# First attention chunk of a block loaded six units ahead, chunks cut at block ends, outputs held in a free buffer

## The chip, the cores and the metric

The kernel runs on one core of one Trainium2 chip. The time is the device time of one execution, in microseconds (us). Five engines work side by side, each with its own queue that it takes in order: PE (TensorE, matmuls; PEld is its weight load), DVE (VectorE), ACT (ScalarE), POOL (GpSimd) and SP (SyncE, which here only starts DMAs).

## The reference

Attention on 4 batches x 8 heads x 576 positions x 64 in two parts that are added: a dense attention on means of four positions (144 x 144), and a local one in which each position sees the 7 positions around it. The result, 2304 tokens x 512, goes through two feed-forward nets:

```python
out_d = sm_attn(q_d, k_d, v_d)             # means of 4 positions
mask = np.abs(pos[:, None] - pos[None, :]) < 4
x = np.repeat(out_d, 4, axis=2) + sm_attn_masked(q, k, v, mask)
g = x @ w_gate; x = (g * sigmoid(g) * (x @ w_val)) @ w_out      # d_ff 1536
h = x @ w_in;   x = (h * clip(h + 3, 0, 6) / 6) @ w_out2         # d_ff 2048
```

## The kernel before

**Blocks and units.** The 2304 tokens are 36 groups of 64, nine to a batch, and `BLOCKS = [8, 6, 8, 8, 6]` cuts them into five blocks, B0 to B4 below. Each block goes through the same 68 units (`NU`), one per 128 columns of a weight matrix: 36 of the first net (G, V, and O which sums into x2), then 32 of the second (H, and P which sums into the output). `run_unit` (L873) issues a unit's matmuls: each weight and each activation is split into a high and a low part, so a unit has 12 matmuls (9 for a P unit of a 6-group block). The first 36 units are called the first half of the block, the other 32 the second half.

**Weights.** `prefetch(i)` (L215) keeps them coming: a load 8 units ahead in B0 (from the 8-byte inputs, turned to f32 by `decode_a` on ACT and `decode_b` on DVE, and written back to DRAM as `kept`), 6 units ahead in later blocks (from `kept`), and two units ahead `split_unit` (L206): ACT writes the high part `wr`, then DVE the low part (in B1 every fourth one is POOL's). The loads sit in SP's queue.

**Attention of the next block beside the nets of this one.** Batch 0 is done before everything else by `first_batch`. The rest of the local attention is done in chunks of 3 groups (`CT = 12` positions of each of 16 x 8 segments), nine of them, on DVE: `chunk_scores` (L726) has two large instructions per group (the product `pr` L731, the sum L734) and a few small ones per chunk; then one Exp on ACT; then `unit_values` (L752) per group: the product `pv` L766 and three sums L770 to L772, with four small instructions ahead of a chunk's first group. `step_x` (L777) turns a group's result on PE and DVE adds the dense part to it (`xf` L796). `CHUNKS = [2, 3, 2, 2, 0]` says how many chunks a block begins: 6, 9, 6, 6 and 0 groups. A block's values must reach to the end of the next block (`limit`), that is 5, 8, 8 and 6 groups; values left over are done first in the next block. Scores are spread over a block's first half, values over the second (`sizes`, L1000). The means for the dense part of the next batch are summed on POOL in the first half (`down_sums` L262, two buffers), its matmuls are in the second half.

**Order.** The program is written unit by unit, but the framework's planner orders each engine's queue from its own estimate of the durations, so work on DVE can come well before its place in the program. DMAs issued through `late` keep their order on SP. A chunk's q, k and v are loaded by `load_chunk` (L690), the first at unit 0 of its block and the second at unit 4 (`CLOAD`), later ones after the scores of the chunk two before. k has 2 buffers, v 3.

**Outputs.** The last P unit ends four sums (three in a 6-group block); `put_out` (L945) copies each from PSUM to one of two buffers `os`, ACT and DVE in turn, and SP writes it out. The third copy waits until the first output has landed.

**Constants.** Two small masks, `ones_last`, are made on POOL and DVE right after `first_batch` (L667 to L685), in a pool that takes over the memory of `first_batch`.

Of the kernel before, what the change touches and what calls it, by code (L numbers as in the profile page):

```python
# [10 lines left out]
F32 = mybir.dt.float32  # L11
# [29 lines left out]
def tile_kernel(  # L41
# [25 lines left out]
    UT = 4 * NSEG  # L67
    CT = 12
    SUB = 4
    NCH = SL // CT  # L70
    UPC = CT // 4
    BS = H * S * D
# [24 lines left out]
    half1 = cp.tile([P, 1], F32, name="half1")  # L97
    nc.gpsimd.memset(half1, 0.5)

    def flat(ap, off, dims):  # L100
# [565 lines left out]
    ap = ctx.enter_context(tc.tile_pool(name="ap", bufs=2))  # L666
    ones_last = []  # L667
    for side in range(2):
        ih = ap.tile([P, H], F32, tag=f"ih{side}", name=f"ih{side}", bufs=1)
        nc.gpsimd.memset(ih, 0.0)  # L670
        nc.gpsimd.affine_select(
            out=ih, in_=ih, compare_op=ALU.not_equal, fill=NEG,
            base=-(NSEG - 1) * side, pattern=[[-NSEG, H]], channel_multiplier=1,
        )
        ind = ap.tile([P, 1], F32, tag=f"ind{side}", name=f"ind{side}", bufs=1)
        nc.vector.tensor_reduce(ind, ih, axis=AX.X, op=ALU.add)
        on = ap.tile([P, 4, W], F32, tag=f"on{side}", name=f"on{side}", bufs=1)
        nc.gpsimd.memset(on, 0.0)
        sgn = 1 if side == 0 else -1
        nc.gpsimd.affine_select(  # L680
            out=on, in_=on, compare_op=ALU.is_ge, fill=1.0,
            base=-3 if side == 0 else 6, pattern=[[sgn, 4], [sgn, W]], channel_multiplier=0,
        )
        nc.vector.tensor_scalar(on, on, ind[:, 0:1], None, op0=ALU.mult)
        ones_last.append(on)  # L685

    odT = {}
    kvq = {}

    def load_chunk(b, c):  # L690
        t0 = c * CT
        qt = ap.tile([P, CT, D], F32, tag="qt", name=f"q{b}_{c}")
        late(nc.sync, qt, flat(q, b * BS + t0 * D, [[PS, P], [1, CT * D]]).rearrange("p (t d) -> p t d", d=D))
        res = [qt]
        NT = CT + 6
        for nm, src in (("k", k), ("v", v)):
            kt = ap.tile([P, NT, D], F32, tag=nm + "t", name=f"{nm}{b}_{c}", bufs=2 if nm == "k" else 3)
            base = b * BS + (t0 - 3) * D

            def ld(p0, p1, r0, r1, shift=0):  # L700
                late(
                    nc.sync, kt[p0:p1, r0:r1, :],
                    flat(src, base + p0 * PS + r0 * D + shift, [[PS, p1 - p0], [1, (r1 - r0) * D]]).rearrange(
                        "p (t d) -> p t d", d=D
                    ),
                )

            if b == B - 1 and c == NCH - 1:
# [16 lines left out]

    def chunk_scores(b, c):  # L726
        qt, kt, vt = kvq.pop((b, c))
        sc = ap.tile([P, CT, W], F32, tag="sc", name=f"sc{b}_{c}", bufs=3)
        for a in range(0, CT, SUB):
# [8 lines left out]
        if c == NCH - 1:  # L738
            nc.vector.tensor_tensor(sc[:, CT - 4:CT], sc[:, CT - 4:CT], ones_last[1], op=ALU.add)
        mx = ap.tile([P, CT], F32, tag="mx", name=f"mx{b}_{c}")  # L740
        nc.vector.tensor_reduce(mx, sc, axis=AX.X, op=ALU.max)
        nc.vector.tensor_tensor(sc, sc, mx[:, :, None].to_broadcast([P, CT, W]), op=ALU.subtract)
        pes[b, c] = sc, vt

    def chunk_exp(b, c):
        sc, _ = pes[b, c]
        nc.scalar.activation(sc, sc, AF.Exp, scale=0.125)
# [4 lines left out]
    def unit_values():  # L752

        b, c, i = vq.popleft()
        pe, vt = pes[b, c]
        if i == 0:
            sm = ap.tile([P, CT], F32, tag="sm", name=f"sm{b}_{c}")
# [3 lines left out]
            nc.vector.tensor_tensor(pe, pe, sm[:, :, None].to_broadcast([P, CT, W]), op=ALU.mult)  # L761
            os_[b, c] = ap.tile([P, CT, D], F32, tag="o", name=f"o{b}_{c}", bufs=3)
# [9 lines left out]
        nc.vector.tensor_tensor(o[:, a:a + SUB], pr[:, :, 0], pr[:, :, 1], op=ALU.add)  # L772
        xq.append((b, c, i, o))
        if i == UPC - 1:
            del pes[b, c], os_[b, c]

    def step_x(limit):  # L777

        if not xq or xq[0][0] not in down_done or xq[0][0] * NG + xq[0][1] * UPC + xq[0][2] >= limit:
            return  # L780
        b, c, i, o = xq.popleft()
        u = c * UPC + i
        gu = b * NG + u
# [177 lines left out]

    chunks = [(b, c) for b in range(1, B) for c in range(NCH)]
    assert sum(CHUNKS) == len(chunks)
    at = 0
# [8 lines left out]
    for bi in range(NB):  # L973
        mine = chunks[at:at + CHUNKS[bi]]
        at += len(mine)
# [13 lines left out]
        def second_half():  # L989
            for ch in mine:  # L990
                chunk_exp(*ch)
                vq.extend((*ch, i) for i in range(UPC))
# [6 lines left out]
        done = (at - len(mine)) * UPC  # L999
        sizes = [len(vq) + len(mine) * UPC, max(min(limit - NG, at * UPC) - done, 0)]  # L1000
        main = iter(())
# [5 lines left out]
        for i in range(bi * NU, (bi + 1) * NU):  # L1007
# [60 lines left out]
```

## Time and profile before

| | |
|---|---|
| median of 3 runs | 1026.6 us (1026.35 to 1028.46) |
| the profiled execution: its time, its span | 1027.78 us, 1025.7 us |
| mean granted TensorE clock | 0.982 of full speed |
| busy share of the span: PE, PEld, DVE, ACT, POOL | 95%, 78%, 77%, 52%, 14% |
| instructions on PE, DVE, ACT, POOL | 4798, 1251, 1070, 130 |
| moved by DMA | 159.92 MB, mean 156 GB/s |

Busy shares are means over the whole span. The five blocks have different limits: the first unit of B1 starts at 283.88 us, of B2 at 464.08, of B3 at 680.80 and of B4 at 874.59, and the second half of B1 at about 380, of B2 at about 578, of B3 at 784. In a row, "idle before <-X" in square brackets is how long the engine stood still before the instruction and whose end released it.

### The profile page before, as it was taken

To read this page: it belongs to the slowest core of one execution; us is meant where nothing else is said; L and a number is where in the kernel's file an instruction comes from. 1 tells how busy PE (TensorE), PEld (TensorE's weight loads), DVE (VectorE), ACT (ScalarE), POOL (GpSimd) and SP (SyncE) were. 2 spreads that over 40 slices of the span, in tenths; PEclk is the share of its full clock that TensorE was granted. 3 is DMA by queue.
4 is the path that set the end of the run, shared out by engine and by line. 5 is a ranking of instruction groups with operands and counts; after the bars stand their busy time and mean duration, and the time that the engine had idled before them with its cause. 6 is when DMAs were issued, how large, how long until landed. Compare 5 with 4: busy or idle time off the path is not lost.

```text
span 1025.7 us, 13478 instructions
## 1 busy us (share of the span) xinstructions
PE 969.7 (95%) x4798; PEld 800.8 (78%) x4800; DVE 789.5 (77%) x1251; ACT 530.9 (52%) x1070; POOL 139.1 (14%) x130
## 2 busy tenths in 40 slices
PE   7868999999997899998999999999999999999996
PEld 4556888777886897886767777777888888999995
DVE  6596999998789999996999765549995655545653
ACT  4684576776544456553344555444435444444553
POOL 5273000000057411211640000000000000000000
PEclk9789999999999899999999999999999999999999
DMA  8668988678486642236833322254223222533331
GB/s 163 175 206 299 332 294 274 210 253 264 143 274 166 181 127 100 102 104 167 234 117 103 103 69 75 82 177 172 91 94 103 82 103 86 161 123 124 126 126 46
DMA packets 82790, 159.92 MB, mean 156 GB/s; under 512 B 19364, under 2 KB 51620, under 8 KB 82724
## 3 DMA queue, kind: packets, MB, share of 16 engines
q1 hardware_dynamic: 77828, 141.25, 44.3%
q10 hardware_dynamic: 4896, 17.83, 4.7%
q8 instruction: 38, 0.62, 0.2%
q14 instruction: 28, 0.23, 0.1%
HBM read 136.51 MB, written 22.54 MB: 155 GB/s over the span
## 4 chain that ended last, share of the span: by engine, by line
PE 68%; DVE 17%; DMA 6%; issue 4%; POOL 2%; ACT 2%; SPq 0%; DVEq 0%; ACTq 0%; POOLq 0%
PE pH L887 19%; PE aP L929 17%; PE aO L929 11%; PE pG L887 9%; PE pV L887 9%; DVE wr L212 4%; DVE sc L734 2%; DVE pr L731 2%; DMA k<-in_k_dram 1%; PE pS L816 1%; DMA out_dram<-os 1%; DVE gV L905 1%; DMA nv<-in_v_dram 1%; DVE sl L899 1%; DVE xf L796 1%
## 5 line engine op out<-in xcount | busy, mean ns | idle before, releaser
L212 DVE TENSOR_TENSOR wr<-w,wr 128x512 fp32r<-128x512 f32 x323 | 234.4, 729 | 85.9 <-ACT wr L209 83.7
L209 ACT ACTIVATE wr<-w 128x512 fp32r<-128x512 f32 x340 | 211.5, 626 | 154.1 <-PE aP L929 68.3
L887 PE MATMUL pH<-x,wr 128*128 128x512 f32 (+1 forms) x960 | 216.1, 376 | 0.4 <-ACT x L942 0.3
L929 PE MATMUL aP<-wr,gH 128*128 128x512 f32 x864 | 213.5, 398 | 0.0
L887 PEld LDWEIGHTS pH<-x,wr 128*128 128x128 f32 x960 | 173.0, 188 | 29.5 <-issue 4.5
L929 PEld LDWEIGHTS aP<-wr,gH 128*128 128x128 f32 x864 | 159.5, 188 | 36.5 <-issue 1.9
L887 PE MATMUL pG<-xr,wr 128*128 128x512 f32 (+3 forms) x732 | 164.3, 378 | 19.5 <-DVE sl L899 14.2
L887 PEld LDWEIGHTS pG<-xr,wr 128*128 128x128 f32 x732 | 134.7, 192 | 43.2 <-issue 12.6
L887 PE MATMUL pV<-xr,wr 128*128 128x512 f32 (+1 forms) x720 | 159.6, 376 | 5.3 <-DVE wr L212 2.2
L929 PE MATMUL aO<-gV,wr 128*128 128x512 f32 (+1 forms) x720 | 158.0, 375 | 3.8 <-DVE wr L212 3.7
L887 PEld LDWEIGHTS pV<-xr,wr 128*128 128x128 f32 x720 | 132.6, 190 | 26.9 <-DVE wr L212 3.5
L929 PEld LDWEIGHTS aO<-gV,wr 128*128 128x128 f32 x720 | 132.8, 190 | 23.9 <-DVE wr L212 5.0
L902 ACT ACTIVATE h<-pH,half 128x512 f32<-128x512 f32 (+1 forms) x80 | 51.6, 645 | 75.8 <-PE pH L887 75.5
L903 DVE SCALAR_TENSOR_TENSOR h<-h,pH 128x512 f32<-128x512 f32 (+1 forms) x80 | 50.5, 631 | 51.5 <-ACT h L902 51.2
L904 ACT ACTIVATE gV<-sl 128x512 fp32r<-128x512 f32 (+1 forms) x60 | 35.3, 588 | 73.5 <-DVE sl L899 73.2
L212 POOL TENSOR_TENSOR wr<-w,wr 128x512 fp32r<-128x512 f32 x17 | 26.9, 1581 | 285.0 <-ACT wr L209 285.0
L731 DVE TENSOR_TENSOR pr<-q,k 128x1792 f32<-128x1792 f32 x27 | 58.9, 2182 | 7.9 <-DMA k<-in_k_dram 7.9
L189 ACT ACTIVATE top<-w 128x512 f16<-128x512 bf16 x68 | 53.4, 789 | 21.8 <-DMA w<-in_moe_w_val_dram 7.7
L893 ACT ACTIVATE sl<-pG 128x512 f32<-128x512 f32 (+1 forms) x60 | 33.1, 552 | 50.0 <-PE pG L887 49.7
L766 DVE TENSOR_TENSOR pv<-sc,v 128x1792 f32<-128x1792 f32 x27 | 55.5, 2057 | 0.3
L904 ACT ACTIVATE gH<-h 128x512 fp32r<-128x512 f32 (+1 forms) x80 | 47.2, 589 | 16.4 <-DVE h L903 14.5
L734 DVE TENSOR_REDUCE sc<-pr 128x28 f32<-128x1792 f32 x27 | 54.3, 2011 | 0.0
(126 smaller groups left out, 852.5 us busy)
## 6 DMA issues: line engine op xcount, KB each, us to landing
w<-kept SPq DMA_DIRECT2D x136, 512.0 KB
kept<-w ACTq DMA_DIRECT2D x34, 512.0 KB
w<-in_moe_w_out_dram SPq DMA_DIRECT2D x28, 512.0 KB
w<-in_moe_w_in_dram SPq DMA_DIRECT2D x16, 512.0 KB
w<-in_moe_w_gate_dram SPq DMA_DIRECT2D x12, 512.0 KB
w<-in_moe_w_val_dram SPq DMA_DIRECT2D x12, 512.0 KB
k<-in_k_dram SPq DMA_DIRECT2D x8, 576.0 KB
v<-in_v_dram SPq DMA_DIRECT2D x8, 576.0 KB
```

Of the source, the lines that this page charges most:

```text
L189: behind(nc.scalar.activation(halves(top[i % 2], 2, F16)[:, :, 1], h3.bitcast(BF16), AF.Copy))
L209: behind(nc.scalar.activation(r[:, 0], s, AF.Copy))
L212: behind(eng.tensor_tensor(r[:, 1], s, r[:, 0].bitcast(F32), op=ALU.subtract))
L731: nc.vector.tensor_tensor(pr, qt[:, a:a + SUB, None, :].to_broadcast([P, SUB, W, D]), win(kt, a, SUB), op=ALU.mult)
L734: nc.vector.tensor_reduce(sc[:, a:a + SUB], pr, axis=AX.X, op=ALU.add)
L766: nc.vector.tensor_tensor(pr, pe[:, a:a + SUB, :, None].to_broadcast([P, SUB, W, D]), win(vt, a, SUB), op=ALU.mult)
L887: nc.tensor.matmul(ps[:, cs], r[:, a, c], x[:, c, b_, cs], start=part is HIGH and a == c == 0, stop=part is LOW and c == NC - 1,)
L893: nc.scalar.activation(sl, ps, AF.Silu)
L902: nc.scalar.activation(h, ps, AF.Relu, scale=1 / 6, bias=half1[:, 0:1])
L903: nc.vector.scalar_tensor_tensor(h, h, 1.0, ps, op0=ALU.min, op1=ALU.mult)
L904: nc.scalar.activation(g[:, 0, :nt], h, AF.Copy)
L929: nc.tensor.matmul(ps, **one, start=f_ == 0 and a == b_ == 0, stop=f_ == nf - 1 and b_ == 1,)
```

## The change

The chunks are cut anew, so that a block's chunks end where the next block does: `CUTS` holds the groups of each chunk, 5, 8, 8 and 6 in all, in 2, 4, 3 and 2 chunks. No values are left over, so both halves of a block have the same number of groups. A chunk keeps its buffers' size (3 groups). At unit 62 of each block the first chunk of the next is loaded. v has 4 buffers and the scores `sc` 4. Outputs are copied into four (three) parts of one tile that has x2's only buffer; x2 was last read by the H units. The masks are made before `first_batch`.

```diff
-CHUNKS = [2, 3, 2, 2, 0]
+CUTS = [[3, 2], [2, 2, 2, 2], [3, 2, 3], [3, 3], []]
-OSB = 2
+EARLY = 6
...
+    ones_last = []          # the same lines as before, pool cp, ahead of first_batch
...
-            kt = ap.tile([P, NT, D], F32, tag=nm + "t", name=f"{nm}{b}_{c}", bufs=2 if nm == "k" else 3)
+            kt = ap.tile([P, CT + 6, D], F32, tag=nm + "t", name=f"{nm}{b}_{c}", bufs=2 if nm == "k" else 4)
...
     def put_out(bi, e, ps):
-        os = sp.tile([P, DM], F32, tag="os", name=f"os{bi}_{e}", bufs=OSB)
+        if e == 0:
+
+            done = sp.tile([P, NC, 2, UMAX * UT], F32R, tag="x2", name=f"os{bi}", bufs=1).bitcast(F32)
+            state["os"] = done.rearrange("p c a t -> p (c a t)")
+        os = state["os"][:, e * DM:(e + 1) * DM]
...
         def first_half():
-            while vq:
-                unit_values()
-                yield
             for m, ch in enumerate(mine):
...
-            while vq and vq[0][0] * NG + vq[0][1] * UPC + vq[0][2] < limit:
+            while vq:
                 unit_values()
                 yield
-        sizes = [len(vq) + len(mine) * UPC, max(min(limit - NG, at * UPC) - done, 0)]
+        sizes = [sum(CUTS[bi])] * 2
...
             next(main, None)
+            if m == NU - EARLY:
+                load_ahead(at + 1)
             step_x(limit)
```

## Rows read from the trace of the kernel before

**Rows 1.** Windows: busy us of each engine (x instructions), PEclk, DMA share, GB/s
```profile
96.00:136.00 40.00, 40.00 (x176) 32.23 (x175) 38.27 (x49) 25.56 (x43) 0.00 (x0) 1.00 1.00 349
...
284.00:380.00 96.00, 82.98 (x452) 79.77 (x451) 92.49 (x99) 43.60 (x79) 46.62 (x33) 0.96 0.61 187
380.00:464.00 84.00, 81.90 (x447) 68.15 (x446) 81.87 (x160) 48.43 (x118) 12.04 (x7) 1.00 0.31 102
464.00:578.00 114.00, 106.36 (x455) 83.23 (x454) 102.05 (x127) 45.58 (x78) 31.69 (x24) 0.99 0.51 152
578.00:676.00 98.00, 98.00 (x473) 75.58 (x472) 59.36 (x127) 52.40 (x116) 0.00 (x0) 1.00 0.24 81
```

**Rows 2.** Chain that ended last: start us, us, engine, tile, line, instructions
```profile
700.31 5.59 PE pV L887 x24
```

**Rows 3.** Timeline, start of B0: start us, us, engine, line, operation [idle before <-releaser]
```profile
88.39 0.26 POOL L680 TENSOR_SCALAR_AFFINE_SELECT on<-on 128x28 f32<-128x28 f32 x1
88.48 0.16 DVE L676 TENSOR_REDUCE ind<-ih 128x1 f32<-128x8 f32 x1 [5.31 <-POOL ih L671]
91.23 4.33 PE L887 MATMUL pG<-xr,wr 128*128 128x512 f32 x12 [5.10 <-DVE sl L899]
...
92.64 0.55 SPq L169 DMA_DIRECT2D w<-in_moe_w_val_dram  x1
...
105.36 0.80 ACT L189 ACTIVATE top<-w 128x512 f16<-128x512 bf16 x1 [2.38 <-DMA w<-in_moe_w_val_dram]
...
112.77 5.76 PE L887 MATMUL pV<-xr,wr 128*128 128x512 f32 x24
...
114.97 0.69 DVE L212 TENSOR_TENSOR wr<-w,wr 128x512 fp32r<-128x512 f32 x1
```

**Rows 4.** Timeline of DVE, first microseconds
```profile
6.71 1.36 DVE L416 TENSOR_SCALAR tmp<-fTq 128x288 f32<-128x288 f32 x2 [5.54 <-PE fTq L410]
```

**Rows 5.** Windows of the instructions on tile pr (scores): DVE busy, PEclk, DMA, GB/s
```profile
284.00:380.00 96.00, 40.65 (x18) 0.96 0.61 187
...
464.00:578.00 114.00, 24.15 (x12) 0.99 0.51 152
```

**Rows 6.** The same of the instructions on tile pv (values)
```profile
380.00:464.00 84.00, 30.83 (x28) 1.00 0.31 102
464.00:578.00 114.00, 26.56 (x27) 0.99 0.51 152
```

**Rows 7.** Lines, DVE, first half of B1: busy us, mean ns
```profile
L742 DVE TENSOR_TENSOR sc<-sc,mx 128x84 f32<-128x84 f32 x3 | 2.9, 957 | 0.0
```

**Rows 8.** Timeline around the start of B2, by engine
```profile
469.87 0.64 SPq L105 DMA_DIRECT2D k<-in_k_dram  x1
...
470.66 5.84 PE L887 MATMUL pV<-xr,wr 128*128 128x512 f32 x24 [0.84 <-ACT sl L893]
...
477.69 2.02 DVE L731 TENSOR_TENSOR pr<-q,k 128x1792 f32<-128x1792 f32 x1 [4.83 <-DMA k<-in_k_dram]
...
480.37 4.34 PE L887 MATMUL pG<-xr,wr 128*128 128x512 f32 x12 [3.87 <-DVE sl L899]
```

**Rows 9.** Timeline of PE, start of B3
```profile
692.86 3.07 PE L887 MATMUL pG<-xr,wr 128*128 128x512 f32 x12 [0.56 <-DVE sl L899]
697.29 3.02 PE L887 MATMUL pG<-xr,wr 128*128 128x512 f32 x12 [1.36 <-DVE sl L899]
```

**Rows 10.** Timeline, last microseconds
```profile
1009.37 8.53 PE L929 MATMUL aP<-wr,gH 128*128 128x512 f32 x36
...
1020.00 0.60 ACT L950 ACTIVATE os<-aP 128x512 f32<-128x512 f32 x1 [4.26 <-DMA out_dram<-os]
```

**Rows 11.** Timeline, first H unit of B0 and the last parts of its x2
```profile
179.97 1.93 PE L887 MATMUL pH<-x,wr 128*128 128x512 f32 x6
...
180.53 0.57 ACT L942 ACTIVATE x<-aO 128x512 fp32r<-128x512 f32 x1
```

**Rows 12.** Timeline of DVE, end of B1: a value of a group that B2 begins with
```profile
460.95 2.02 DVE L766 TENSOR_TENSOR pv<-sc,v 128x1792 f32<-128x1792 f32 x1
```

More of the change, by code (lines that the diff above doesn't have):

```diff
@@ L67, in tile_kernel @@
     UT = 4 * NSEG
-    CT = 12
     SUB = 4
-    NCH = SL // CT
-    UPC = CT // 4
+    CT = SUB * max(chain(*CUTS))
     BS = H * S * D
@@ L98, in tile_kernel @@
     nc.gpsimd.memset(half1, 0.5)
+    ones_last = []
+    for side in range(2):
+        ih = cp.tile([P, H], F32, tag=f"ih{side}", name=f"ih{side}")
+        nc.gpsimd.memset(ih, 0.0)
+        nc.gpsimd.affine_select(
+            out=ih, in_=ih, compare_op=ALU.not_equal, fill=NEG,
+            base=-(NSEG - 1) * side, pattern=[[-NSEG, H]], channel_multiplier=1,
+        )
+        ind = cp.tile([P, 1], F32, tag=f"ind{side}", name=f"ind{side}")
+        nc.vector.tensor_reduce(ind, ih, axis=AX.X, op=ALU.add)
+        on = cp.tile([P, 4, W], F32, tag=f"on{side}", name=f"on{side}")
+        nc.gpsimd.memset(on, 0.0)
+        sgn = 1 if side == 0 else -1
+        nc.gpsimd.affine_select(
+            out=on, in_=on, compare_op=ALU.is_ge, fill=1.0,
+            base=-3 if side == 0 else 6, pattern=[[sgn, 4], [sgn, W]], channel_multiplier=0,
+        )
+        nc.vector.tensor_scalar(on, on, ind[:, 0:1], None, op0=ALU.mult)
+        ones_last.append(on)
     def flat(ap, off, dims):
@@ L666, in tile_kernel, with load_chunk @@
     ap = ctx.enter_context(tc.tile_pool(name="ap", bufs=2))
[L667 to L685, printed above, removed]
     odT = {}
     kvq = {}
-    def load_chunk(b, c):
-        t0 = c * CT
+    def load_chunk(b, c, n):
+        t0 = c * SUB
+        ct = n * SUB
         qt = ap.tile([P, CT, D], F32, tag="qt", name=f"q{b}_{c}")
-        late(nc.sync, qt, flat(q, b * BS + t0 * D, [[PS, P], [1, CT * D]]).rearrange("p (t d) -> p t d", d=D))
+        late(
+            nc.sync, qt[:, :ct],
+            flat(q, b * BS + t0 * D, [[PS, P], [1, ct * D]]).rearrange("p (t d) -> p t d", d=D),
+        )
         res = [qt]
-        NT = CT + 6
+        NT = ct + 6
         for nm, src in (("k", k), ("v", v)):
-            kt = ap.tile([P, NT, D], F32, tag=nm + "t", name=f"{nm}{b}_{c}", bufs=2 if nm == "k" else 3)
+            kt = ap.tile([P, CT + 6, D], F32, tag=nm + "t", name=f"{nm}{b}_{c}", bufs=2 if nm == "k" else 4)
             base = b * BS + (t0 - 3) * D
@@ L706, in ld @@
                 )
-            if b == B - 1 and c == NCH - 1:
+            if b == B - 1 and c + n == NG:
                 ld(0, P, 0, NT - 3)
@@ L724, in tile_kernel, with chunk_scores @@
     down_done = set()
-    def chunk_scores(b, c):
+    def chunk_scores(b, c, n):
         qt, kt, vt = kvq.pop((b, c))
-        sc = ap.tile([P, CT, W], F32, tag="sc", name=f"sc{b}_{c}", bufs=3)
-        for a in range(0, CT, SUB):
+        ct = n * SUB
+        sc = ap.tile([P, CT, W], F32, tag="sc", name=f"sc{b}_{c}", bufs=4)[:, :ct]
+        for a in range(0, ct, SUB):
             pr = ap.tile([P, SUB, W, D], F32, tag="pr", name=f"pr{b}_{c}_{a}", bufs=1)
@@ L752, in unit_values @@
     def unit_values():
-        b, c, i = vq.popleft()
+        b, c, n, i = vq.popleft()
         pe, vt = pes[b, c]
         if i == 0:
-            sm = ap.tile([P, CT], F32, tag="sm", name=f"sm{b}_{c}")
+            ct = n * SUB
+            sm = ap.tile([P, CT], F32, tag="sm", name=f"sm{b}_{c}", bufs=1)[:, :ct]
             nc.vector.tensor_reduce(sm, pe, axis=AX.X, op=ALU.add)
@@ L772, in unit_values @@
         nc.vector.tensor_tensor(o[:, a:a + SUB], pr[:, :, 0], pr[:, :, 1], op=ALU.add)
-        xq.append((b, c, i, o))
-        if i == UPC - 1:
+        xq.append((b, c + i, i, o))
+        if i == n - 1:
             del pes[b, c], os_[b, c]
     def step_x(limit):
-        if not xq or xq[0][0] not in down_done or xq[0][0] * NG + xq[0][1] * UPC + xq[0][2] >= limit:
+        if not xq or xq[0][0] not in down_done or xq[0][0] * NG + xq[0][1] >= limit:
             return
-        b, c, i, o = xq.popleft()
-        u = c * UPC + i
+        b, u, i, o = xq.popleft()
         gu = b * NG + u
@@ L959, in put_out @@
             nc.sync.dma_start(dst, os[n * UT:(n + m) * UT, :])
-    chunks = [(b, c) for b in range(1, B) for c in range(NCH)]
-    assert sum(CHUNKS) == len(chunks)
+    chunks = []
+    b, u = 1, 0
+    for n in chain(*CUTS):
+        chunks.append((b, u, n))
+        u += n
+        assert u <= NG
+        if u == NG:
+            b, u = b + 1, 0
+    assert b == B
     at = 0
@@ L991, in second_half @@
                 chunk_exp(*ch)
-                vq.extend((*ch, i) for i in range(UPC))
-            while vq and vq[0][0] * NG + vq[0][1] * UPC + vq[0][2] < limit:
+                vq.extend((*ch, i) for i in range(ch[2]))
+            while vq:
                 unit_values()
```

15 lines of the change are left out of this document (7 added, 8 removed).

## The prediction

> **What bounds the kernel now.** I read first the chain that ended last, then the busy time by window for each half of a block, then the timelines at the places where PE stood still. Where nothing disturbs it, PE needs 5.59 us for 24 matmuls of an 8-group block [rows 2], 2.79 us per unit of 12; in a 6-group block the matmuls have three quarters of the columns, and I estimate 2.10 us. The reader is to see in the windows [rows 1] where it gets that. The second half of B2 is PE's: PE busy 98.0 of 98.0 us, DVE 59.4. The first half of B1 is DVE's: it should last 36 x 2.10 = 75.6 us and about 2 us of small matmuls, it lasts 96, and DVE is busy for 92.5 of them. B1's second half is close to both limits (81.9 busy on each of 84.0). B2's first half should last 36 x 2.79 = 100.4 and about 1.2, and lasts 114; DVE is busy for 102. So the losses that this change can touch lie on DVE and at block starts, and the rest is PE time that it doesn't touch.
>
> **The change part by part.**
>
> *Constants first.* At 83 us DVE meets the first mask instruction in its queue and waits 5.31 us for POOL, which is behind its sums for batch 1. Behind it stands the product that frees PE's bank, so PE waits 5.10 us, and its next 12 matmuls take 4.33 us where 2.79 is normal [rows 2, 3]: the clock had dropped. That makes 5.10 + 1.54 = 6.6 us. What is late next? From 96 to 136 us the DMA engines are busy for the whole time at 349 GB/s [rows 1]. ACT stands 2.38 us at 105.36 for a weight load, and the chain from such loads ends in the low part of a weight written at 114.97 + 0.6 (it ends at 115.7, and DVE starts the next one 0.6 after each start), while PE wants it at 112.77 + 2.8 = 115.6 [rows 3]. There is no slack there: PE can't be earlier than those loads. They come earlier only by what the shorter second chunk leaves out: 2 groups instead of 3 are 36 rows instead of 48 (q 8 for 12, k and v 14 for 18), 12 x 256 B x 128 partitions = 0.39 MB, or 1.1 us at 349 GB/s. I take 1.5 us, with ends 0 and 6.6. At the front, the moved instructions are eight on POOL, the longest 0.26 us [rows 3], and four on DVE of 0.2 us or less; DVE stands idle for 5.54 us until 6.71 [rows 4]. The work behind them on POOL (masks for batch 0) comes at most 8 x 0.26 = 2.1 us later; nearest to rows 4 I take 0, and keep 2.1 as the far end.
>
> *Chunks cut at block ends.* The scores per block go from 6, 9, 6, 6 groups to 5, 8, 8, 6. In B1 a score group costs DVE 40.65 / 9 = 4.52 us [rows 5], a value group 30.83 / 7 = 4.40 us [rows 6]. Before, B1 did 9 scores and, by its queue, also the values of the two groups that belong to B2's start (the second of them starts at 460.95, [rows 12]; its sums end after 464), so nearly 9 values with its own 7. Now it has 8 and 8. That takes 4.5 and, as part of the left-over work ran past 464, some 4.0 us off DVE; a fourth chunk adds six small instructions, between 0.2 us each and the 0.96 us that L742 shows when it meets POOL [rows 7], 1.2 to 5.7 us; I take 1.2, since five of the six are a few columns wide. Net 7.3. DVE is busy in B1 for 92.5 + 81.9 = 174.4 of 180.0 us, so nearly all of it shows in the time, and the two shortest PE stalls save a clock drop: I take 7.5 us. Ends: 0, if the planner fills the room with scores of B2, which can now be early; 12, if the slower clock of that stretch (0.96 over 96 us, worth 3.8) goes as well.
>
> B2 gets two more scores in its first half, 2 x 24.15 / 6 = 8.1 us [rows 5], and loses nothing on paper: its second half has to take more values. But before, the planner had already pulled 27 value instructions, nearly seven groups, into this first half [rows 6]; it fills DVE whatever there is. With more scores fewer values fit, and the others fall to the second half, where DVE is idle for 98.0 - 59.4 = 38.6 us; four values there are 17.6 us. So the two scores cost nothing as long as that cover is there; if they came on top of a full DVE they would cost 8.1 us.
>
> B2's POOL sums run beside these scores. A score cost 4.52 us in B1 with POOL busy 46.6 us, and 4.03 in B2 with 31.7 [rows 1, 5]. The Trainium skill (page "SBUF — State Buffer", section "Who interferes with whom") says that a VectorE instruction with two SBUF inputs and a GpSimd instruction that reads SBUF exclude each other for a whole instruction, which speaks against more scores beside the sums. By that rule the two added scores would be priced as in B1, and B2's term below would be 2 x 0.49 = 1.0 us smaller; by the row it isn't.
>
> *First chunk early.* At B2's start q, k and v stand on SP behind the outputs: k is issued at 469.87 and DVE, which has the first score next in its queue, waits 4.83 us until 477.69 [rows 8]. Behind that score stand the gate product and the weight splits, so PE waits 3.87 us and then runs 12 matmuls in 4.34 instead of 2.79 us: 3.87 + 1.55 = 5.4 us. At B3's start the same order costs PE 0.56 + 1.36 = 1.9 us [rows 9]. At B1's start the gap is part of the DVE time above. At unit 62 the three loads go ahead of the outputs, of two weight loads and of the next block's first sums for the dense part on SP; the issue of one takes 0.64 us [rows 8], so these come some 2 us later, and weights are loaded 6 units (12.6 to 16.7 us) ahead, so nobody waits. Their buffers are free: q's and k's last readers are in the block's first half, and v has a fourth buffer. Six units before the end are 12.6 us or more against the 7.8 us from 469.87 to 477.69. I take the whole 5.4 and 1.9.
>
> *Outputs in x2's buffer.* The third copy no longer waits for the first output. At B2's start the gate function stands behind that copy on ACT, and PE waits 0.84 us for it [rows 8]: 0.8 us. At the very end PE is done at 1009.37 + 8.53 = 1017.9 and the third copy starts at 1020.0, when the first output has landed [rows 10]: 2.1 us, straight off the end; I take 2.0, since three outputs now overlap. Whether the copies would wait for each other's DMAs, as all go to one tile: x2 is such a tile, and PE read its first part at 179.97 before its third was written at 180.53 [rows 11], so parts are told apart, and I cost this at nothing.
>
> **Sum.** 1.5 (B0) + 7.5 (B1) + 5.4 + 0.8 (B2) + 1.9 (B3) + 2.0 (end) = 19.1 us. The profiled execution took 1027.8 us, so 1008.7; it stands 1.2 us above the median of the runs shown, so 1007.5 against that.
>
> **The rivals.**
>
> 1. *DVE stays full.* The planner puts the freed time of B1 to use for scores of B2, and only the waits go: 1.5 + 0 + 6.2 + 1.9 + 2.0 = 11.6 us, 1015. For it: nearly seven value groups were pulled ahead in B2. Against: those early scores then don't burden B2.
> 2. *All of it and more.* The start of B0 comes back whole (6.6) and B1 gets its 12: 6.6 + 12 + 6.2 + 1.9 + 2.0 = 28.7, 998. For it: nothing but the size of the gaps; against: the full DMA engines from 96 us.
> 3. *The wait moves to the block's end, and the kernel is slower.* The planner now believes k to be there while the last units of the block before run, and puts the first score among them. If k lands later than it thinks, DVE stands there with the splits of the next weights behind it. PE has two units' weights in hand, 2 x 2.79 = 5.6 us, so it decides from a DVE wait of 5.6 us. The load took 7.8 us in a quiet stretch; the weight load issued at 92.64, when DMA was full, was waited for until 105.36 [rows 3], 12.7 us. A k as late as that stalls PE for 12.7 - 5.6 + 1.5 (the clock drop) = 8.6 us at each of the three boundaries, 25.8; the old waits are gone all the same. All three: 1026.6 + 25.8 - 19.1 = 1033; with B1's freed time refilled too, 1041; one alone, 1016, is inside the forecast's spread. For it: DVE was put before a late k in B2 already. Against: DMA is 24% busy in the second half of B2 [rows 1].
> 4. *It does not do what it says*: the early k is waited for as long as before, DVE is refilled, and B0 gains nothing; only 0.8 + 2.0 remain, 1024, and a bad schedule of DVE takes them back.
>
> **How the numbers follow.** The forecast has 0.57, with a range of its own from 1002 to 1013. Rival 1 has 0.22, rival 2 0.08, rival 3 0.08, rival 4 0.05. The range that leaves out no more than 2 in 10 goes from 999 to 1022: outside it are rivals 3 and 4, half of rival 2 and some 0.03 of the rest. What a measurement of this kernel can tell from no change is 0.2%, 2 us. Faster by more than that: the forecast and rivals 1 and 2, 0.87. Within 0.2%: rival 4, 0.05. Slower: rival 3, 0.08.
>
> **What would show it.** No wait of DVE for the mask at 83 us, but waits of ACT or PE for weight loads between 95 and 120 us instead (if PE runs through there, rival 2). The first half of B1 near 88 us. No DVE wait for k at a block's start and none in the last six units of the block before (rival 3 otherwise). More `pv` in B2's second half, with PE still full there. The third copy right behind the last matmul at the end. The forecast is wrong if B1's two halves together still last over 177 us, or if PE loses over 2 us in B2's second half.

## The result and the profile after

The changed kernel takes 1016.6 us (median of 4 executions, 1015.1 to 1020.8), the kernel before 1027.5 beside it: a ratio of 0.9891 with an interval of 0.9844 to 0.9937. Timed once more on another chip (e8 below) the ratio was 0.9888, from 0.9867 to 0.9909. So the change is worth 11 to 12 us (9 to 14 by the second interval), where the sum said 19.1; the time lies in the wide range, beside rival 1's number, and outside the forecast's own 1002 to 1013.

The starts of the first matmuls of each half, from the PE timelines, give the lengths below (us; "a" is the half of G, V and O, "b" that of H and P; the profiled executions took, row by row, 1027.8, 1015.1, 1015.2, 1012.7, 998.7, 1021.7, 1012.5 and 1015.4 us; the last six rows are runs of the experiments below).

| | up to B1 | B1a | B1b | B2a | B2b | B3a | B3b | B4 and end |
|---|---|---|---|---|---|---|---|---|
| before | 283.9 | 96.0 | 84.2 | 113.8 | 102.9 | 103.0 | 90.6 | 151.3 |
| after | 283.2 | 90.3 | 85.3 | 109.9 | 103.7 | 100.4 | 90.6 | 149.8 |
| after again (e8) | 283.3 | 88.4 | 85.3 | 111.4 | 104.2 | 100.4 | 90.6 | 149.8 |
| before, no POOL sums (e10) | 282.0 | 86.7 | 84.2 | 108.9 | 102.9 | 103.9 | 90.7 | 151.3 |
| after, no POOL sums (e7) | 284.6 | 79.1 | 85.3 | 103.0 | 104.1 | 100.4 | 90.6 | 149.8 |
| after, no early chunk (e3) | 280.9 | 89.8 | 84.3 | 112.2 | 105.0 | 106.9 | 90.7 | 150.1 |
| after, two early chunks (e4) | 287.1 | 84.3 | 85.6 | 108.3 | 103.8 | 100.6 | 90.7 | 150.2 |
| after, Exp held back (e5) | 283.8 | 90.4 | 85.3 | 103.5 | 109.0 | 100.8 | 90.7 | 150.1 |

On the page of the changed kernel (busy us, share of the span and instructions; then the chain's shares by engine) PE is busy for 95%:

```profile
PE 965.3 (95%) x4798; PEld 800.9 (79%) x4800; DVE 796.3 (79%) x1263; ACT 536.7 (53%) x1076; POOL 135.1 (13%) x130
...
PE 66%; DVE 20%; DMA 5%; issue 5%; ACT 2%; POOL 2%; SPq 1%; DVEq 0%; ACTq 0%
```

Against [rows 1], the windows of the changed kernel (us, busy time of PE, PEld, DVE, ACT, POOL with instructions, granted clock, DMA share, GB/s) are these:

```profile
283.23:373.54 90.31, 81.00 (x449) 77.69 (x448) 84.00 (x95) 44.22 (x78) 43.72 (x33) 0.98 0.58 187
373.54:458.81 85.27, 82.75 (x449) 68.63 (x449) 82.90 (x161) 50.39 (x120) 11.26 (x7) 1.00 0.36 122
458.81:568.72 109.91, 103.66 (x449) 83.37 (x448) 95.74 (x117) 48.54 (x79) 31.00 (x24) 0.98 0.47 152
568.72:672.42 103.70, 103.70 (x498) 79.84 (x497) 81.05 (x156) 54.65 (x121) 0.00 (x0) 1.00 0.29 95
```

DVE is busy in B1 for 84.0 + 82.9 = 166.9 us, 7.5 less than the 174.4 of before; but the two halves together are only 4.6 us shorter. In B2's second half DVE is busy for 81.1 us, where it was 60.8 (59.4 in the shorter window of [rows 1]): it took nearly three values and two of B3's scores, and PE stayed full.

What went out of B1 is not what was forecast. Against [rows 5], these are the windows of the scores (tile `pr`, two instructions per group) in B0's second half and B1's two halves of the changed kernel:

```profile
179.81:283.23 103.42, 9.15 (x4) 1.00 0.67 223
283.23:373.54 90.31, 25.77 (x12) 0.98 0.58 187
373.54:458.81 85.27, 4.03 (x2) 1.00 0.36 122
```

Two of B1's eight scores ran in B0's second half, where none ran before and where the early k let them, and one of B2's ran in B1: seven scores, 29.8 us, in place of nine, 40.65. The scores alone took 10.9 us off DVE in B1, and its busy time fell by only 7.5, because other instructions got longer. The 12 low parts of the gate in B1's first half took 8.5 us before and take 13.1 (line, engine, operation, shapes, count, busy us, mean ns, idle before; the changed kernel's row stands at e7):

```profile
L905 DVE TENSOR_TENSOR gV<-sl,gV 128x384 fp32r<-128x384 f32 x12 | 8.5, 708 | 0.0
```

The start of B0, in the timeline of the changed kernel (start, us, engine, line, operation, idle time before and what ended it), answers to [rows 3]:

```profile
90.39 3.02 PE L892 MATMUL pG<-xr,wr 128*128 128x512 f32 x12 [0.16 <-DVE sl L904]
...
103.67 0.80 ACT L208 ACTIVATE top<-w 128x512 f16<-128x512 bf16 x1 [1.48 <-DMA w<-in_moe_w_val_dram]
...
111.71 5.84 PE L892 MATMUL pV<-xr,wr 128*128 128x512 f32 x24 [0.96 <-ACT sl L898]
```

PE's wait for the masks fell from 5.10 to 0.16 us. The next V units begin 1.1 us earlier than before (111.71 for 112.77), and ACT still waits for a weight load; from 96 to 136 us the DMA engines are busy for 0.97 of the time, at 335 GB/s.

The start of B2, SP, DVE, ACT and PE of the same timeline, answers to [rows 8]:

```profile
469.90 2.83 SPq L124 DMA_DIRECT2D nq<-in_q_dram  x2
473.72 0.42 SPq L124 DMA_DIRECT2D k<-in_k_dram  x1
...
479.45 2.02 DVE L736 TENSOR_TENSOR pr<-q,k 128x1792 f32<-128x1792 f32 x1 [3.79 <-DMA k<-in_k_dram]
...
488.70 1.28 ACT L752 ACT_TABLE_LOAD   x1
497.01 0.25 ACT L752 ACTIVATE sc<-sc 128x56 f32<-128x56 f32 x1 [7.02 <-DVE sc L747]
...
499.22 7.24 PE L892 MATMUL pV<-xr,wr 128*128 128x512 f32 x24 [5.41 <-ACT sl L898]
```

This is the row to read longest. The first chunk's k is no longer waited for. But the second chunk's k is issued at 473.72, behind the sums' loads; DVE waits 3.79 us for it; ACT has the Exp of that chunk in its queue ahead of the next gate function, waits 7.02 us for its scores, and PE waits 5.41 us for the gate and then takes 7.24 us for 24 matmuls instead of 5.59 [rows 2]. In the window behind the wait the granted clock is 0.50, the lower of its two levels (1.2 GHz):

```profile
499.00:502.00 3.00, 2.78 (x7) 2.23 (x8) 1.29 (x2) 1.99 (x5) 1.16 (x1) 0.50 0.21 64
```

The end answers to [rows 10]; the third copy now starts 0.03 us after the last matmul, which ends at 998.12 + 8.53 = 1006.65:

```profile
998.12 8.53 PE L934 MATMUL aP<-wr,gH 128*128 128x512 f32 x36
...
1006.68 0.60 ACT L959 ACTIVATE os<-aP 128x512 f32<-128x512 f32 x1 [2.19 <-PE aP L934]
```

### The profile page after: what moved, and what is told of

It is laid out like the page before. It is cut to its first block, busy times and chain, and to the rows that moved or that the text cites. A ratio compares the mean times of both kernels' runs of the same rounds, so it can differ in the third digit from the quotient of the medians.

```text
span 1013.1 us, 13506 instructions
## 1 busy us (share of the span) xinstructions
PE 965.3 (95%) x4798; PEld 800.9 (79%) x4800; DVE 796.3 (79%) x1263; ACT 536.7 (53%) x1076; POOL 135.1 (13%) x130
## 4 chain that ended last, share of the span: by engine, by line
PE 66%; DVE 20%; DMA 5%; issue 5%; ACT 2%; POOL 2%; SPq 1%; DVEq 0%; ACTq 0%
PE pH L892 17%; PE aP L934 16%; PE aO L934 10%; PE pV L892 9%; PE pG L892 9%; DVE wr L231 5%; DVE sc L739 2%; DVE pr L736 2%; DVE gV L910 1%; DVE w L217 1%; DMA k<-in_k_dram 1%; DVE xf L801 1%; PE pS L821 1%; DVE gH L910 1%; DVE sl L904 1%
## 5 line engine op out<-in xcount | busy, mean ns | idle before, releaser
L231 DVE TENSOR_TENSOR wr<-w,wr 128x512 fp32r<-128x512 f32 x323 | 233.0, 725 | 84.3 <-ACT wr L228 81.8
L892 PE MATMUL pG<-xr,wr 128*128 128x512 f32 (+3 forms) x732 | 160.4, 374 | 3.4 <-DVE wr L231 3.3
L736 DVE TENSOR_TENSOR pr<-q,k 128x1792 f32<-128x1792 f32 x27 | 58.3, 2159 | 11.0 <-DMA k<-in_k_dram 10.8
```

Of the source, the lines that this page charges most:

```text
L231: behind(eng.tensor_tensor(r[:, 1], s, r[:, 0].bitcast(F32), op=ALU.subtract))
L736: nc.vector.tensor_tensor(pr, qt[:, a:a + SUB, None, :].to_broadcast([P, SUB, W, D]), win(kt, a, SUB), op=ALU.mult)
L892: nc.tensor.matmul(ps[:, cs], r[:, a, c], x[:, c, b_, cs], start=part is HIGH and a == c == 0, stop=part is LOW and c == NC - 1,)
```

## The experiments

**e1, the constants alone** (the kernel before with the masks built at the front).

```diff
+    ones_last = []          # behind half1, in the pool of the constants
+    for side in range(2):
...
     ap = ctx.enter_context(tc.tile_pool(name="ap", bufs=2))
-    ones_last = []
-    for side in range(2):
```

> The kernel before with one edit: the masks are made ahead of first_batch. Theory: the DVE wait for POOL at 83 us goes (5.31 us), but PE cannot use it, since the DMA engines are full from about 92 to 136 us and the weights of the next units come when they come; the first H unit of B0 still starts within 1.5 us of 180 us, and the whole is within 2 us of the kernel before. Rival: PE gets the 6.6 us back, H starts near 174 us and the whole is 5 to 7 us faster.

Measured: ratio 0.9982 (0.9968 to 0.9997), 1.9 us (0.3 to 3.3). B0's second half begins at 177.4 for 180.0, but in the profiles of this case that start lies anywhere from 177.4 to 184.1, so the ratio decides. The stall of 6.6 us doesn't come back as 6.6.

**e2, the outputs alone** (the kernel before with the four outputs in x2's buffer).

```diff
-        os = sp.tile([P, DM], F32, tag="os", name=f"os{bi}_{e}", bufs=OSB)
+        if e == 0:
+            done = sp.tile([P, NC, 2, UMAX * UT], F32R, tag="x2", name=f"os{bi}", bufs=1).bitcast(F32)
+            state["os"] = done.rearrange("p c a t -> p (c a t)")
+        os = state["os"][:, e * DM:(e + 1) * DM]
```

> The kernel before with one edit: outputs are copied into x2's buffer. Theory: the third copy no longer waits for the first output to land; the end comes 1.5 to 2 us earlier and B2 starts without the 0.84 us wait of PE, 2 to 3 us in all. Rival: copies into one tile wait for each other's DMAs, or ACT's freed time only meets the next wait, and the whole is the same or slower by up to 5 us.

Measured: 0.9993 (0.9975 to 1.0011), not told from nothing: 0.7 us, from 1.1 slower to 2.6 faster, so the expected 2 to 3 are not shown and not quite ruled out. In the profile the last block with its end is 1.4 us shorter, but the profiled execution reached B1 3.6 us later than the one of before. So the end is read from the rows, not from this ratio; nothing shows the copies waiting for each other's transfers.

**e3, no early chunk** (the changed kernel without the load at unit 62).

```diff
-            if m == NU - EARLY:
-                load_ahead(at + 1)
```

> The changed kernel without the early load: new cuts, outputs in x2's buffer, masks first, but each block's first chunk is loaded at its unit 0. Theory: the cuts alone take a score and most of a value off DVE in B1, 4 to 5 us, and the outputs 2 to 3 us, while DVE waits for k at the starts of B1, B2 and B3 as before and PE loses some 5 us in B2 and 2 us in B3 to it: 1019 to 1022 us, 4 to 6 us slower than the changed kernel. Rival: the cuts do nothing (the planner refills DVE) and all beyond the outputs comes from the early load: 1023 to 1026 us. Second rival: the wait only moved from the first chunk to the second, so the early load is worth nothing: 1015 to 1017 us.

Measured: 0.9940 (0.9920 to 0.9960), so the early load is worth some 5 us of the change's 11.5, good to about 3 by the two intervals. All eight scores of B1 stay in its first half here, and B1 takes 174.2 us, 6.0 less than before: so B1's gain doesn't need the early load. At B3's start DVE waits 6.70 us for k in this kernel, and B3's first half takes 106.9 us, 3.9 more than in the kernel before.

**e4, two early chunks.**

```diff
-                load_ahead(at + 1)
+                load_ahead(at + 2)
```

> The changed kernel with the first two chunks of the next block loaded at unit 62 instead of one. Theory: in B2 of the changed kernel DVE waits 3.79 us for the second chunk's k, which stands behind two loads for the sums on SP, ACT's Exp of that chunk waits 7.0 us behind DVE, and the gate function behind the Exp stops PE for 5.41 us with 1.6 us of slower clock after it; with the second chunk there in time this goes, B2's first half lasts 103 to 104 us instead of 110, and the whole is near 1009 us (6 to 8 us faster than the changed kernel). Rival: DVE is simply full at B2's start, with two more scores beside POOL's sums; then the Exp is as late as before, PE still stops for 4 to 6 us there, and the whole is within 2 us of the changed kernel.

Measured: 0.9826 (0.9809 to 0.9844), 6 us better than the changed kernel. The size is the expected one, the place only in part. B2's first half still took 108.3 us, since PE waited for POOL's sums there, in which POOL had waited for their load (timeline of PE):

```profile
477.55 0.62 PE L303 MATMUL pqT<-ident,dnq 72*128 72x72 f32 x3 [3.06 <-POOL dnq L291]
```

By the half lengths more than half of the gain lies in B1's first half, which the expectation doesn't name: 84.3 us for 90.3 and 88.4 in the changed kernel. POOL does the same sums there and is busy for 45.8 us, DVE does as many scores, and yet DVE is busy for 78.5 us in place of 84.0. Two of these three groups of its instructions are shorter than in the changed kernel (its rows stand at e7), the score products are longer; first the window:

```profile
287.06:371.38 84.32, 79.58 (x450) 76.77 (x449) 78.53 (x98) 46.45 (x81) 45.79 (x33) 1.00 0.58 185
```

```profile
L231 DVE TENSOR_TENSOR wr<-w,wr 128x512 fp32r<-128x512 f32 x26 | 20.0, 777 | 2.1 <-ACT wr L228 2.1
L736 DVE TENSOR_TENSOR pr<-q,k 128x1792 f32<-128x1792 f32 x6 | 14.4, 2402 | 3.2 <-DMA k<-in_k_dram 3.2
L910 DVE TENSOR_TENSOR gV<-sl,gV 128x384 fp32r<-128x384 f32 x12 | 8.2, 682 | 0.0
```

**e5, the Exp behind the gates** (the changed kernel; k stays late, one Exp in B2 is held behind the sixth gate function of that block by an edge that sets the order on ACT alone).

```diff
-        nc.scalar.activation(sc, sc, AF.Exp, scale=0.125)
+        e = nc.scalar.activation(sc, sc, AF.Exp, scale=0.125); (b, c) == (2, 7) and behind_gate(e)
```

> The changed kernel with one edge added: the Exp of B2's second chunk (L752) stays behind the sixth gate function of that block on ACT; up to that point all queues are as in the changed kernel. Theory: DVE's wait for the second chunk's k (3.79 us) costs PE 5.4 us only because this Exp stood ahead of the gate functions on ACT and waited 7.02 us for DVE. Then PE's wait of 5.41 us at 499.22 goes or falls below 2 us, B2's first half falls from 110.0 to 104.5 to 106.5 us, and the time is 4 to 6 us below that of the changed kernel run beside it. Rival: DVE is what is late, whatever ACT does (behind the score stand the gate product and the splits): then PE waits the same 3 to 5 us at the place for DVE instead of ACT, B2's first half stays within 1.5 us of 110, and the time within 1.5 us.

Measured: 0.9832 (0.9807 to 0.9856), 4.7 us below the changed kernel beside it (1011.7 for 1016.4). DVE, ACT and PE at the same place in its timeline:

```profile
480.61 2.03 DVE L736 TENSOR_TENSOR pr<-q,k 128x1792 f32<-128x1792 f32 x1 [4.01 <-DMA k<-in_k_dram]
...
485.96 2.82 PE L934 MATMUL aO<-gV,wr 128*128 128x512 f32 x11 [0.82 <-DVE wr L231]
...
494.75 5.62 PE L892 MATMUL pV<-xr,wr 128*128 128x512 f32 x23 [0.15 <-DVE wr L231]
...
497.85 0.25 ACT L752 ACTIVATE sc<-sc 128x56 f32<-128x56 f32 x1 [0.98 <-DVE sc L747]
```

DVE waits for k as long as ever (4.01 us), and PE for 0.82 and 0.15 us. B2's first half took 103.5 us. The late k alone costs PE about a microsecond here (0.82 + 0.15); with the Exp ahead of the gates it costs 5.4 and the clock. In the profiled execution, the slowest of five, B2's second half then took 109.0 us; e9 to e12 come back to that.

**e6, both:** two early chunks and the Exp behind the gates.

> The first two chunks of each block loaded early, and the same edge for the Exp in B2. With both chunks early this Exp waited for nothing in the profile (its start 473.22 had no idle time before it) and PE's 3.06 us at 477.55 were for POOL's sums. Theory: the edge adds nothing to the second early chunk; both remove the same stall: within 2 us of the version with two chunks early (ratio 0.9826, about 1011). Rival: the Exp with its two table loads delays gates there too, and the time falls 3 us or more below 1011.

Measured: 0.9834 (0.9815 to 0.9853), as e4 and e5 each: the gains don't add up. The stall of 5.41 us is gone in all three. B1's first half took 84.9 us, as in e4, but B2's 106.9, as PE again waited for POOL's sums (3.62 us); in e5, whose second chunk comes late, it took 103.5.

**e7, the changed kernel without POOL's sums.**

```diff
-            nc.gpsimd.tensor_tensor(t[:, :, 0:2], t[:, :, 0:2], t[:, :, 2:4], op=ALU.add)
-            nc.gpsimd.tensor_tensor(dn[w][:, half, hh * 4:hh * 4 + 4], t[:, :, 0], t[:, :, 1], op=ALU.add)
+            if tag == "nat":
+                nc.gpsimd.memset(dn[w][:, half, hh * 4:hh * 4 + 4], 0.5)
+            else:
+                ...
```

> The changed kernel without POOL's sums for the dense part of batches 2 and 3 (L290, L291): a memset of the result on POOL stands in their place, so the dense part of these batches is not that of the reference. All other work stays, but the planner orders the engines anew. Theory: B1's first half lasts 90.3 instead of about 83 us because DVE and POOL hold each other up: the 27 low-part splits (L231) take 985 ns there and the 12 gate low parts (L910) 1102 ns, where 690 and 560 are the undisturbed ones, 8.0 + 6.5 us on DVE. Without the sums (some 30 of POOL's 43.7 us in that half) L231 falls to 700 to 780 ns and L910 to 560 to 650, DVE's busy time in that half from 84.0 to 70 to 74 us, and the half to 82 to 85 us (PE has 81.0 us of matmuls there); B2's first half falls by 2 to 4 us too, and the time to 1003 to 1009 on a scale where the kernel before has 1028. Rival: the half is held by something else (late weights on ACT, the order of DVE's queue): DVE's busy time falls the same way, but the half stays above 88 us and the time within 3 us of the changed kernel.

Measured: 0.9708 (0.9691 to 0.9726), 18 us below the changed kernel. The dense part of two batches is left out here. First the costliest DVE instructions of B1's first half with the sums, in the changed kernel (line, engine, operation, shapes, count, busy us, mean ns, idle before), then without them:

```profile
L231 DVE TENSOR_TENSOR wr<-w,wr 128x512 fp32r<-128x512 f32 x27 | 26.4, 985 | 4.5 <-ACT wr L228 4.4
L736 DVE TENSOR_TENSOR pr<-q,k 128x1792 f32<-128x1792 f32 x6 | 13.7, 2288 | 0.2 <-issue 0.2
L910 DVE TENSOR_TENSOR gV<-sl,gV 128x384 fp32r<-128x384 f32 x12 | 13.1, 1102 | 0.0
L739 DVE TENSOR_REDUCE sc<-pr 128x28 f32<-128x1792 f32 x6 | 12.0, 2006 | 0.0
```

```profile
L231 DVE TENSOR_TENSOR wr<-w,wr 128x512 fp32r<-128x512 f32 x27 | 19.0, 711 | 7.2 <-ACT wr L228 7.1
L739 DVE TENSOR_TENSOR pr<-q,k 128x1792 f32<-128x1792 f32 x6 | 12.1, 2017 | 0.2 <-issue 0.2
L742 DVE TENSOR_REDUCE sc<-pr 128x28 f32<-128x1792 f32 x6 | 12.1, 2010 | 0.0
L913 DVE TENSOR_TENSOR gV<-sl,gV 128x384 fp32r<-128x384 f32 x12 | 7.5, 638 | 0.0
```

The same numbers of splits, score products and gate low parts take 7.4 + 1.6 + 5.6 = 14.6 us less. The reduction, which reads one tile, is the same in both. That is no fixed price of the sums: e4, with all of them, has DVE busy for 78.5 us in this half, 8.2 above e7, and the changed kernel for 84.0, 13.7 above it. So the order of the queues, by which DVE's and POOL's instructions meet, decides a good part of it. And the half is now PE's (windows of B1's two halves and of B2's first):

```profile
284.55:363.60 79.05, 77.58 (x449) 76.85 (x448) 70.27 (x95) 44.60 (x78) 16.23 (x17) 1.00 0.69 213
363.60:448.90 85.30, 82.79 (x449) 68.62 (x449) 82.90 (x161) 50.34 (x120) 12.34 (x11) 1.00 0.36 122
448.90:551.91 103.01, 102.16 (x449) 82.26 (x448) 89.94 (x118) 48.68 (x79) 0.00 (x0) 1.00 0.53 163
```

So the 18 us are the worth of leaving out the sums and of the new order together: the stall of 5.41 us in B2 is gone here too (PE's only wait in that half is 0.9 us), and e5, with all the sums, takes 103.5 us for that half.

**e8, the changed kernel again.**

> The changed kernel once more, as it is, beside the others of this call, to have their times against it on one chip, and to see how far its halves vary from one execution to the next. Theory: a half of a block varies by less than 1.5 us between two executions (the order on each engine is fixed), so that the 90.3 us of B1's first half and the 5.4 us stall in B2 show again. Rival: they are chance of one execution, and one of them is off by more than 3 us.

Measured: 1016.4 us, 0.9888. The stall in B2 is there again, 5.4 us long and on the same instruction. B1's first half took 88.4 us this time, 1.9 less, and its splits 923 ns for 985: between the two statements, so a length of that half is good to 2 us only.

**e9, the sums' first loads early** (e6, and at unit 62 also the first two loads of the next dense sums).

```diff
                 load_ahead(at + 2)
+                if bi + 2 < B:
+                    load_down(bi + 2, "q", 0, 0, ap, "nat", 2, nc.sync)
+                    load_down(bi + 2, "q", 0, 1, ap, "nat", 2, nc.sync)
```

> The version with two early chunks and the Exp behind the gates, and beside them the first two loads of the next block's dense sums (nq, L124) issued at unit 62, behind the early chunks, instead of behind the outputs at the block's start. In the version without this PE waits 3.62 us at 475.70 for POOL's sums, which wait for that load, and the matmuls behind run at the lower clock (PEclk 0.98 over 106.9 us). Theory: this is the last stall at B2's start that a late load causes; it goes, B2's first half falls from 106.9 to 102.5 to 104 us (PE has 102.2 us of work there), and the time by 3 to 5 us, ratio to the kernel before 0.978 to 0.981. Rival: POOL's sums then run earlier, beside the early scores and the last units of the block before, and hold DVE up there: the second halves of B1 (87.2) and B0 grow by 2 us or more and the time stays within 1.5 us of 1012.

Measured: 0.9816 (0.9788 to 0.9843), not told from e6. B2's first half took the 103.5 us that the theory says, and the time was still not won. Part of it is given back in B0's second half, the rival's place: 104.7 us here, and 106.2 and 105.9 in e11 and e12, which have the same early loads, for 103.4 in e6. PE waits longer for DVE at its end, first in e6, then here:

```profile
278.46 4.67 PE L934 MATMUL aP<-wr,gH 128*128 128x512 f32 x19 [1.23 <-DVE gH L910]
```

```profile
280.69 4.69 PE L935 MATMUL aP<-wr,gH 128*128 128x512 f32 x19 [2.45 <-DVE gH L911]
```

B2's second half took 109.1 us here. There, in the timeline of PE and in windows around it:

```profile
565.00 1.72 PE L893 MATMUL pH<-x,wr 128*128 128x512 f32 x3 [1.56 <-DVE x L949]
```

```profile
564.00:567.00 3.00, 1.80 (x5) 0.91 (x6) 3.00 (x6) 0.24 (x1) 0.00 (x0) 0.92 0.00 0
567.00:570.00 3.00, 3.00 (x9) 2.24 (x8) 3.00 (x6) 2.10 (x4) 0.00 (x0) 0.50 0.48 178
570.00:573.00 3.00, 3.00 (x8) 2.32 (x8) 2.93 (x4) 1.24 (x3) 0.00 (x0) 0.50 0.03 5
```

A wait of 1.56 us, then six microseconds at 0.50, the lower of the two levels (1.2 GHz).

**e10, the kernel before without POOL's sums** (the edit of e7).

> The kernel before, without POOL's sums for the dense part of batches 2 and 3, as they were left out of the changed kernel (a memset stands in their place; the dense part of these batches is not that of the reference). Without them the changed kernel had a first half of B1 of 79.1 us with DVE busy for 70.3 (84.0 with them), B2's first half of 103.0, and ratio 0.9708. Theory: POOL held DVE up in the kernel before as well (wr 948 ns, pr 2508 ns for 2018 in B1's first half), by some 14 us; without the sums that half falls from 96.0 to 80 to 84 us, close to PE's 77.6, so that most of what the new cuts save on DVE there would be worth nothing: the change is then worth some 8 to 12 us in all, and this kernel's ratio is 0.979 to 0.984. Rival: the kernel before is bound by the amount of DVE's own work, not by POOL; it gains 8 us or less from this (ratio above 0.992), and the first half of B1 stays above 88 us.

Measured: 0.9866 (0.9844 to 0.9888), which neither statement had. Its first half of B1 takes 86.7 us:

```profile
282.00:368.67 86.67, 81.36 (x452) 79.58 (x450) 80.28 (x98) 44.34 (x79) 16.36 (x17) 0.96 0.70 208
```

DVE is busy for 80.3 instead of 92.5 us [rows 1], so the sums cost it 12 us of DVE's time before, and 84.0 - 70.3 = 13.7 in the changed kernel. Beside e7 the change is worth 0.9708 / 0.9866 = 0.984 where there are no sums: 16 us (12 to 20, from the ends of the two intervals), against 11.5 (9 to 14) with them; the two ranges overlap. By the half lengths the difference isn't in B1, which gains 6.5 us without the sums (170.9 to 164.4) and 4.6 and 6.5 with them. It is in B2's first half, 5.9 us for 3.9 and 2.5, where the changed kernel has its stall of 5.41 us and e7 hasn't.

**e11 and e12, the value product behind x2** (e9, with the first value product of batch 3 held behind the last addition for B2's second half; e12 is e9 again beside it).

```diff
-        nc.vector.tensor_tensor(
+        pv = nc.vector.tensor_tensor(
             pr, pe[:, a:a + SUB, :, None].to_broadcast([P, SUB, W, D]), win(vt, a, SUB), op=ALU.mult
-        )
+        ); (b, c, i) == (3, 0, 0) and behind_gate(pv, ("x2", 2))
```

> The version with the early sums loads, and one more edge on DVE: the first value product of batch 3 (pv, 2.02 us) stays behind the last addition of x (the input of B2's second half). In the version without it B2's first half lasted 103.5 us, but in its profile this product stood between the first and the second addition, PE waited 1.56 us for DVE at 565.00, the clock fell to 0.50 from 567 to 573 us, and B2's second half took 109.1 us instead of 103.5 to 104. Theory: the time won in the first half is given back at the half's boundary by that one product; behind the additions the wait goes, the second half takes 103 to 105 us in the profile, the executions above 1012 disappear, and the median falls by 3 to 5 us, to 1006 to 1008.5 (ratio 0.977 to 0.981). Rival: DVE is behind PE at the boundary by its amount of work, not by this one product: PE waits as long for the low parts of the weights or the gates behind it, the second half stays above 107 us and the median above 1010.

> The version with the early sums loads once more, beside the one with the added edge, so that the two are timed on one chip. Both theories: a median within 2 us of 1011.4, with single executions on two levels, some near 1005 and some near 1013; by the theory the low ones are those in which the clock does not fall at the boundary of B2's halves.

Measured: 1009.5 and 1010.3 us, both 0.9825 (0.980 to 0.985). In e11 the second half of B2 took 103.5 us, but in e12, with the product still between the additions, 103.9, and nothing waited there. So the stall at that boundary is a matter of the single execution (the profiles of e5 and e9 had it, those of e6 and e12 not, with the product in the same place), the edge changes nothing that could be told, and executions above 1012 us stayed in e11 too (1013.3).

The versions with two early chunks, the held Exp, or more (e4, e5, e6, e9, e11, e12: 0.9816 to 0.9834) all beat both kernels, by about 6 us against the changed one; none is told from another.

## Why the prediction was right or wrong

**Constants: right within the noise.** Forecast 1.5 us with full DMA engines as the next limit; e1 measured 1.9 (0.3 to 3.3), and the DMA engines are still at 0.97 in the changed kernel. Rival 2's 6.6 didn't come. The 0.6 us by which the two profiles reach B1 earlier settles nothing, as that start differs by more between executions.

**Chunk cuts: the amount came out by luck, and the step to the time fell short.** The forecast took one score and most of a value off B1, 7.3 us of DVE work net, and DVE's busy time there fell by 7.5. But two scores went and not one, as two of B1's had moved into B0's second half and one of B2's had come in, and longer instructions, 4.6 us of gate low parts above all, took the surplus back. Then "nearly all of it shows in the time" held only in part: B1 got 4.6 us shorter in one profile and 6.5 in e8. About 1.1 us of the shortfall is B1's second half, which grew from 84.2 to 85.3 with or without the sums.

The prices were not fixed either. What the DVE rows of B1 priced as DVE's own work was in part time in which POOL held it (12 us before, e10). One such place in the changed kernel (POOL, DVE and PE of the timeline):

```profile
324.56 2.39 POOL L291 TENSOR_TENSOR dnv<-nv 72x256 f32<-72x256 f32 x1
...
326.29 4.11 DVE L231 TENSOR_TENSOR wr<-w,wr 128x512 fp32r<-128x512 f32 x2
326.92 1.26 POOL L231 TENSOR_TENSOR wr<-w,wr 128x512 fp32r<-128x512 f32 x1
...
328.78 5.57 PE L892 MATMUL pV<-xr,wr 128*128 128x384 f32 x23 [3.00 <-DVE wr L231]
```

Two splits of 0.69 us each take 4.11 while POOL works, and PE waits 3.00 us for the second. Such bunches stall PE although DVE has idle time (6.3 us of that half, 3.6 before). Where the sums are gone the half is PE's 77.6 us, the forecast's 75.6 + 2, and the change gives it 7.6 us (e7, e10), but it gives e8 7.6 us with the sums as well (96.0 to 88.4). So it is shown that POOL lengthens DVE's work, and not that POOL took away a part of the gain. How the shortfall of B1's first half divides between such bunches and the planner's order stays open, since every edit that removes sums also reorders the queues, and e4 wins 4 to 6 us there with the sums in place.

The Trainium skill (page "SBUF — State Buffer", section "Who interferes with whom") says that VectorE and GpSimd share a port pair under an exclusive lock. The trace agrees: two-input products are slowed (985 for 711 ns, 1102 for 638) and the one-input reduction isn't (2006 and 2010). The rule also spoke against the added scores in B2, and was right in the direction: the seven score products of B2's first half took 2172 ns each, where the six of before took 2017 and e7's seven, without sums, 2020, 1.1 us in all; the forecast went by the row of before.

**Scores into B2 at no cost: right.** They would have cost 8.1 us on a full DVE. One of the two ran in B2's first half (seven scores for six), the other already in B1. B2's second half grew by 0.8 us (1.3 in e8), PE full in the window above.

**First chunk early: the step that failed most.** "I take the whole 5.4 and 1.9", and 0.8 for the gate: B3's first half gained 2.6 us, more than the 1.9 (two of its six scores now ran in B2), but B2 as a whole 3.1 and 1.1 (the two profiles) instead of 6.2. The wait that the early chunk removed was replaced by one for the next chunk's k, which the prediction never asked about: with the first chunk early, DVE stands at the second chunk's scores from 475.66 us (479.45 - 3.79), 1.9 us after its k was issued. By itself that costs PE little (e5: DVE waits 4.01 us, PE 0.82 and 0.15). It became a PE stall because the planner had put the chunk's Exp ahead of two gate functions on ACT, presumably because by its own estimate k was there. The prediction asked what is queued behind the waiting instruction on DVE, and not what waits for DVE on ACT. Holding back the Exp alone (e5) brings 4.7 us, most of the 7 to 8 that the sum was off by. The second chunk early as well (e4) brings 6, but more than half of it in B1.

**Outputs: about right at the end.** 2.0 forecast, 1.5 in both profiles of the last block with its end; copies don't wait for each other. The 0.8 at B2's start can't be read apart from the stall there, and e2, the edit alone, measured 0.7 us (1.1 slower to 2.6 faster), so the time settles neither.

**The rivals.** Rival 1 had the number (1015) without its mechanism: DVE wasn't refilled in B1, where its busy time fell by 7.5 us and a single score of B2 was pulled in. The sum's number missed its own range by 4 us because B2's stall came back in another form and B1 gave less; that the time lies in the wide range is owed to the room left for rival 1. Rival 3's wait at a block's end was not there: DVE's only wait for k in the last six units, in B2, was 1.35 us, below the 5.6 from which it decides, and PE was full. Of the signs named, the third copy, the full PE in B2's second half, the mask wait, B1's first half near 88 us (90.3 and 88.4) and B1's 175.6 us (below 177) came as said; "no DVE wait for k" didn't (10.8 us in five waits).

## What to carry to other kernels

When a late load is moved ahead, look up the next load of the same kind and ask who meets it, on every engine: an instruction that a planner placed early by its belief about a transfer blocks its in-order queue, and that link can cost more than the wait itself (5.4 us for 1.0 here). A busy time in a stretch where VectorE and GpSimd both work is not an amount of work: price instructions by their undisturbed duration first, and expect the surcharge to change with the order of the queues (8 or 14 us of VectorE time in one half for the same sums here). Where several stalls sit in one stretch, removing one shows the next, so expect part of each gain to come back.

## What the runs showed of the hardware

Without POOL's sums for two batches, and with the queues ordered anew, the changed kernel takes 18 us less (1016.4 to 998.4), though POOL is busy for only 13% of its span and has 2% of the chain. Beside the same sums DVE's low parts of the gate took 682 ns each in one order of the queues (e4) and 1102 in another (the changed kernel), where 638 is the duration without them (e7); the one-input reduction took 2006 to 2010 in all three. A PE wait as short as 1.56 us was followed by some six microseconds at the lower clock in one execution, and in another execution of the same program that wait and that loss were absent (109.1 and 103.9 us for the same half); single executions of one kernel differ by up to 8.7 us here (e5: 1006.8 to 1015.4), so a change of this size needs several.
